# Longformer attention and token mixer, 8 batches: three moves in the turns and scores of batches 1 and 2

## The chip, the cores and the metric

The kernel runs on one core of a Trainium2 chip. The metric is the time of one execution in device microseconds (us), lower is better. The core has a matrix engine (TensorE, PE in the profile, with its weight loads as PEld) and four others that work beside it: VectorE (DVE), ScalarE (ACT), GpSimd (POOL) and SyncE (SP). In this kernel SP only issues transfers, and POOL casts and issues transfers.

## What is computed

Attention with a band of 32 keys to either side and 8 global tokens, then a mixer over the tokens and one over the channels, each with a residual. B=8 batches, H=8 heads, S=576 tokens, D=64.

```python
scores = scale * np.matmul(q, k.transpose(0, 1, 3, 2))
mask = np.abs(pos[:, None] - pos[None, :]) <= window          # window = 32
mask = mask | is_global[:, None] | is_global[None, :]         # 8 global tokens
attn = softmax(np.where(mask, scores, -1e9))
x = (attn @ v)                        # as [8, 576, 512]: the heads side by side
xt = x.transpose(0, 2, 1)
h = np.maximum(xt @ w_tok1, 0.0) @ w_tok2                     # 576 -> 256 -> 576
u = x + h.transpose(0, 2, 1)
h2 = np.maximum(u @ w_ch1, 0.0) @ w_ch2                       # 512 -> 1536 -> 512
return u + h2
```

## The kernel before

Inputs and output are float32, and all matmuls read float16. The 8 heads are worked on as 4 pairs (p = 0 to 3), the 576 tokens as five blocks of 128 (tau = 0 to 4, the last has 64).

There is no loop over batches in time with clean borders. `period(b)` works on two batches at once: the channel products of batch b, and the attention and token mixer of batch n = b + 1, whose loads and casts for batches n + 1 and n + 2 stand there too. The order of the instructions on each engine is the order in which this Python code writes them. The channel products of batch b lie in a list, `dense`: 12 products `M4` (matmuls `b1p`, L713; relu L719 on ACT or L717 on DVE), in odd b three `M4l` for the last 64 tokens of two batches, and per token block two halves of `M5` (six matmuls `op` each, L757; after the second half the sum `osb` on DVE, L761, and its store from SP, L762). `d(k)` writes the next k of them, `d(k, keep)` stops when `keep` are left. So a call of `d` between two steps of the attention puts dense matmuls of batch b between PE instructions of batch n.

The steps of batch n, by their functions, with the names and lines in the profile:

- Casts of q and k: `cast_qk` (L371, tile `qk` from `lq`, `lk`; L368 for the rest of the tokens, `rn` from `lr`). `casts(2, ...)` is a list of nine: the rest, and then q and k of pair 0 (numbers 1, 2), of pair 1 (3, 4), of pair 2 (5, 6), of pair 3 (7, 8). Loads: L88 (`lq`, `lk`), L95 (`lr`), `load_v16` (L360, values).
- Turns: for batches 1 and 2 PE transposes q and k. `T` has eight transposes of one pair into `pT` (L446), `TE_q` and `TE_k` copy them out to `qT` (L450) and `kT` (L456), and `TR` does the rest of the tokens (`pr`, L468 to L470). From batch 3 on transposing transfers do this.
- Scores: `S_all` gives one pair in two PSUM tiles (18 matmuls L486, two exponentials L492 on ACT). `S_two` gives two pairs in three PSUM tiles (36 matmuls L510, four exponentials L516). `SM` masks a pair on DVE (L535, L537 twice).
- Global tokens: `GK` (`gk`, L546 and L547, exponentials `lf`, L549 and L550), `lf_mask` (L557), `OG` (`og`, L564, and `rf` on DVE, L569). `halves` copies values (`vod`, L416 and L418).
- Values: `PV` (`pv`, L590 and L604, normalized on DVE, L619 and L620).
- Token mixer: `M1` (`a1p`, L635, one of five parts each; after the last the relu `a1`, L643, on ACT), `M2` (`hp`, L652, sum `u16`, L657), `M2l` (`hpl`, L664), and `M3_pe` for batch 1 (transposes `pu`, L691, copy `uT`, L693).

PSUM tiles of the attention come from a pool of three buffers (`pss`), those of the dense products from one of two (`psm`). In periods 0 and 1 the scores go pair by pair through `scores(p, k)`, and from batch 3 on through `scores_two(p, k)`. Period 0 is n = 1, period 1 is n = 2.

Of the kernel before, what the change touches and what calls it, by code (L numbers as in the profile page):

```python
# [27 lines left out]
def kernel(  # L28
# [336 lines left out]
    def cast_qk(b, ti, p, eng):  # L365

        if p is None:
            eng(out=rn.rearrange("p n (r d) -> p (n r) d", r=2), in_=lr)  # L368
        else:
            hs = slice(2 * p, 2 * p + 2)  # L370
            eng(out=qk[:, ti, p].rearrange("q i (r d) -> q r i d", r=2), in_=(lq, lk)[ti][:, hs])  # L371
# [41 lines left out]
    def halves(b, cp, c0=0, c1=NT - 1, which=(0, 1)):  # L413
        v0, v1 = vsh[b % 2], vod[b % 2]
        if 0 in which:
            cp(out=v1[0:HB, c0:c1], in_=v0[HB:P, c0:c1])  # L416
        if 1 in which:
            cp(out=v1[HB:P, c0:c1], in_=v0[0:HB, c0 + 1 : c1 + 1])  # L418
# [30 lines left out]
    def TE_q(b, p, copy):  # L449
        copy(  # L450
            out=qTs[b % 2][:, p, 0:4, NG:QS].rearrange("p t (x i) -> p t x i", i=4),
            in_=st[b]["pT", p][:, 0].rearrange("p (i t x) -> p t x i", i=4, t=4),
        )
# [7 lines left out]
    def TE(b, p, copy):  # L461
        TE_q(b, p, copy)
        TE_k(b, p, copy)
# [322 lines left out]
    def period(b):  # L786
# [37 lines left out]

        def scores_two(p, k):
            es = S_two(n, p)
            turned = [] if p else [(f, i) for i in (2, 3) for f in (order_k, order_q)]

            def next_turned():
                if turned:  # L830
                    f, i = turned.pop(0)
                    f(n, i)

            es[0]()
            es[1]()
            next_turned()
            for i in (2, 3):
                d(1)
                es[i]()
                next_turned()  # L840
            SM(n, p)
            d(1)
            next_turned()
            SM(n, p + 1)
            d(1 + k)

        if n > 2:
            scores_two(0, max(tail - 4, 0))
            halves(n, act)
            GK(n)  # L850
            if m < B:
                turns(m)
            d(1)
            lf_mask(n)
            scores_two(2, 1)
        else:
            scores(0, tail > 5)
            scores(1, max(tail - 4 - (tail > 5), 0))
            scores(2, 0)
            GK(n)  # L860
            if n == 2:
                c3 = casts(3, nc.gpsimd.tensor_copy)
                for i in (2, 4):
                    c3[i]()
                load_rest(4, nc.gpsimd)
                for ti in range(2):
                    for i in (5 + ti, 7 + ti):
                        c3[i]()
                    load_qk(4, slice(0, H), nc.gpsimd, slice(ti, ti + 1))
                turns(3)  # L870
            d(1)
            lf_mask(n)
            if n == 1:
                halves(n, dve, 0, 2)
            else:
                halves(n, dve, which=(0,))
            scores(3, 0)
            if n == 1:
                d(1)
            else:  # L880
                halves(n, dve, which=(1,))
            if n == 1:
                c2 = casts(2, nc.scalar.copy)
                for c in c2[0:1] + c2[1::2]:
                    c()
                for p in range(NP):
                    cast_qk(2, 1, p, nc.gpsimd.tensor_copy)
                load(3, nc.sync)
                gather(1)
            else:  # L890
                d(1)
        OG(n)
# [46 lines left out]
            order_q(3, 0)  # L939
        d(1 if n == 1 else len(dense) - (8 + 2 * odd), keep)  # L940
        M1(n, 4)
        d(1, keep)
        if 2 < m < B:
            load_v16(m)
# [10 lines left out]
        if n == 1:  # L955
            d(1, keep)
            M3_pe(1, 0)
            M3_pe(1, 1)
            T(2, 0)
            TE(2, 0, act)  # L960
            TR(2, dve)
            M3_pe(1, 2)
            M3_pe(1, 3)
            T(2, 1)
            d(1, keep)
            TE(2, 1, dve)
            c3 = casts(3, nc.gpsimd.tensor_copy)
            for i in (0, 1, 3):
                c3[i]()
            load_v16(2)  # L970
        else:
            d(1)
            if n == 2:
                order(3, 1)
                gather_c(1)
            d(1)
# [151 lines left out]
```

## Time and profile before

| what | value |
|---|---|
| median of 3 runs | 303.9 us (303.44 to 305.51) |
| profiled execution | 302.77 us, span 300.7 us |
| PE | 289.7 us busy (96%), 2940 matmuls |
| DVE | 180.9 us (60%) |
| ACT | 168.2 us (56%) |
| POOL | 77.3 us (26%) |
| granted TensorE clock | 0.994 |
| transfers | 47.70 MB, mean 159 GB/s |

The profiled execution took 2.07 us more than the span of its instructions. A row of the timeline gives the start in us, the busy time of the group, the engine, the line, the operation with its tiles, shapes and count, and in brackets the idle time ahead of it with what ended it. A row of the list of waits reads: who waited, for whom, us in all, number of waits, mean. A row of the table of stages gives a stretch, its length, the busy us of PE, PEld, DVE, ACT and POOL with the number of instructions, the granted clock, the busy share of the DMA engines and GB/s. Period 0 lies before about 60 us, period 1 from there to about 98 us.

### The profile page before, as it was taken

Reading aid. Unit: us, or ns where it says so; the run is one execution under the profiler, and the core shown is the slowest. Engines: PE = TensorE matmul, PEld = TensorE weight load, DVE = VectorE, ACT = ScalarE, POOL = GpSimd, SP = SyncE. Lnnn points to the kernel's source line nnn. Section 1 sums busy time; section 2 is a strip of 40 time slices with the busy share of each in tenths; the row PEclk is TensorE's granted clock in tenths of the full one; section 3 lists DMA queues with packets and bytes.
Section 4 is the critical chain, followed back from the end, with each engine's and each line's share of the span. In section 5 each row is a group of like instructions: output and inputs, shape, how many; then the busy total and the mean of one; then the engine's idle time right before and its main releaser. Section 6 shows DMA issues by size and latency. Waiting matters only on the chain.

```text
span 300.7 us, 7163 instructions
## 1 busy us (share of the span) xinstructions
PE 289.7 (96%) x2940; PEld 150.0 (50%) x2940; DVE 180.9 (60%) x427; ACT 168.2 (56%) x268; POOL 77.3 (26%) x120
## 2 busy tenths in 40 slices
PE   8869999999999999999999999999999999999994
PEld 7543644354565445444565445444564445444642
DVE  7976698467864845777664755776554766320022
ACT  6785883445638774588539763687343673205500
POOL 8787862289932103200230005000000000000000
PEclk9998999999999999999999999999999999999999
DMA  6999999899999999947993699955502410051013
GB/s 200 238 225 217 264 179 269 233 267 193 239 166 119 150 288 296 164 91 220 297 145 71 177 358 138 91 89 180 101 20 52 159 37 2 17 138 73 0 72 106
DMA packets 106499, 47.70 MB, mean 159 GB/s; under 512 B 84962, under 2 KB 100450, under 8 KB 106466
## 3 DMA queue, kind: packets, MB, share of 16 engines
q1 hardware_dynamic: 67536, 33.18, 48.4%
q0 software_dynamic: 38768, 13.93, 43.9%
q8 instruction: 23, 0.38, 0.6%
q10 hardware_dynamic: 162, 0.13, 0.1%
q14 instruction: 10, 0.08, 0.1%
HBM read 36.11 MB, written 9.44 MB: 151 GB/s over the span
## 4 chain that ended last, share of the span: by engine, by line
PE 84%; DMA 5%; SPq 4%; DVE 3%; ACT 2%; issue 1%; POOLq 0%; ACTq 0%
PE op L757 28%; PE b1p L713 27%; PE a1p L635 5%; PE hp L652 4%; PE b1lp L729 4%; PE pv L590 3%; DMA lq<-in_q_dram 3%; PE pv L604 3%; SPq L102 2%; PE s L510 2%; DMA lv<-in_v_dram 2%; SPq L88 1%; PE pT L446 1%; PE s L486 1%; PE ope L741 1%; PE og L564 1%
## 5 line engine op out<-in xcount | busy, mean ns | idle before, releaser
L713 PE MATMUL b1p<-uT,wc 128*128 128x512 f16 x384 | 92.6, 379 | 0.0
L757 PE MATMUL op<-wc,b 128*128 128x512 f16 x384 | 87.2, 379 | 0.0
L719 ACT ACTIVATE b<-b1p 128x512 f16<-128x512 f32 x84 | 50.2, 598 | 65.6 <-PE b1p L713 50.4
L757 PEld LDWEIGHTS <-b 128*128 128x128 f16 x384 | 36.5, 98 | 43.8 <-issue 1.6
L713 PEld LDWEIGHTS <-wc 128*128 128x128 f16 x384 | 35.3, 98 | 39.5 <-issue 4.0
L360 POOL DMA_DIRECT2D vsh<-in_v_dram x35 | 30.0, 870 | 88.0 <-PE pv L590 76.5
L761 DVE TENSOR_TENSOR osb<-u,op 128x512 f32<-128x512 f16 x32 | 21.9, 685 | 40.4 <-PE op L757 40.4
L657 DVE TENSOR_TENSOR u<-x,hp 128x512 f16<-128x512 f16 x28 | 17.4, 682 | 25.1 <-PE hp L652 25.1
L516 ACT ACTIVATE e_all<-s 128x816 f16<-128x816 f32 (+3 forms) x40 | 24.6, 687 | 7.0 <-issue 4.9
L537 DVE TENSOR_TENSOR e_all<-e_all,bandm 128x616 f16<-128x616 f16 x56 | 24.8, 483 | 1.0
L620 DVE TENSOR_TENSOR x<-pv,rr 128x512 f16<-128x512 f32 x32 | 22.1, 692 | 1.1
L492 ACT ACTIVATE e_all<-s 128x544 f16<-128x544 f32 (+1 forms) x24 | 16.2, 683 | 5.6 <-PE s L486 3.1
L619 DVE RECIPROCAL rr<-pv 128x8 f32<-128x8 f32 (+1 forms) x40 | 8.1, 202 | 17.9 <-PE pv L604 17.7
L371 ACT CAST qk<-lq 128x512 f16<-128x512 f32 x26 | 15.8, 621 | 4.7 <-DMA lq<-in_q_dram 3.8
L635 PE MATMUL a1p<-x,w 128*128 128x512 f16 x64 | 17.5, 392 | 0.0
L590 PEld LDWEIGHTS <-e_all 128*64 128x64 f16 x576 | 12.4, 113 | 8.3 <-issue 6.5
L590 PE MATMUL pv<-vsh,e_all 128*64 128x66 f16 x320 | 14.9, 198 | 0.0
L604 PE MATMUL pv<-rf,lf 128*128 128x264 f16 (+1 forms) x80 | 13.6, 284 | 0.9 <-DVE rf L569 0.8
L371 ACT CAST qk<-lk 128x512 f16<-128x512 f32 x21 | 12.9, 621 | 2.4 <-DMA raw<-qk 1.8
L652 PE MATMUL hp<-a,w 128*128 128x512 f16 x56 | 13.2, 378 | 0.5 <-ACT a L643 0.5
L590 PE MATMUL pv<-vod,e_all 128*64 128x66 f16 x256 | 12.1, 199 | 0.9 <-DVE vod L418 0.9
L717 DVE TENSOR_SCALAR b<-b1p 128x512 f16<-128x512 f32 x12 | 8.3, 691 | 7.4 <-PE b1p L713 6.8
(184 smaller groups left out, 350.5 us busy)
## 6 DMA issues: line engine op xcount, KB each, us to landing
out_dram<-osb SPq DMA_DIRECT2D x32, 256.0 KB, 4.0
lq<-in_q_dram SPq DMA_DIRECT2D x4, 1024.0 KB, 6.5
lk<-in_k_dram SPq DMA_DIRECT2D x4, 1024.0 KB, 7.4
wc<-in_moe_w_ch_dram POOLq DMA_DIRECT2D x6, 512.0 KB, 9.3
vsh<-in_v_dram POOLq DMA_DIRECT2D x21, 128.0 KB, 6.9
lq<-in_q_dram POOLq DMA_DIRECT2D x2, 1024.0 KB, 8.6
lk<-in_k_dram POOLq DMA_DIRECT2D x2, 1024.0 KB, 13.5
vsh<-in_v_dram POOLq DMA_DIRECT2D x14, 96.0 KB, 6.8
```

The lines of the kernel that those rows point to most:

```text
L360: nc.gpsimd.dma_start(out=vsh[b % 2][r0:r1, c, :, 0:D], in_=v[b, :, j0 : j0 + (r1 - r0), :].rearrange("h p d -> p h d"),)
L371: eng(out=qk[:, ti, p].rearrange("q i (r d) -> q r i d", r=2), in_=(lq, lk)[ti][:, hs])
L516: nc.scalar.activation(out=e_all[:, 2 * (p + dp) : 2 * (p + dp) + 2, x0:x1], in_=tiles[t][:, :, o : o + x1 - x0], func=AF.Exp, scale=scale,)
L537: nc.vector.tensor_mul(out=e2[:, par], in0=e2[:, par], in1=bandm)
L590: nc.tensor.matmul(ps[r0 : r0 + HB, hf, VW * hh : VW * hh + VW], lhsT=e_all[:, h, x0 : x0 + HB], rhs=(vsh, vod)[i][b % 2][:, tau, h, :], s ...
L604: nc.tensor.matmul(s["pv", tau][r, hf, 0 : NP * VW], lhsT=s["lf"][:, P * tau : P * tau + (HB if last else P)], rhs=s["rf"][:, 2 * hf : 2 * ...
L620: nc.vector.tensor_tensor(out=x_of(b, tau)[r].rearrange("p (f h x) -> p f h x", f=2, h=NP), in0=pq[r, :, :, 0:D], in1=rr[r].unsqueeze(3).t ...
L635: nc.tensor.matmul(ps[tt], lhsT=w, rhs=x_of(b, ch), start=(ch == 0), stop=(ch == NT - 1))
L652: nc.tensor.matmul(ps[:, i, :], lhsT=w2[:, ch, P * tau : P * tau + P], rhs=s["a1"][:, ch, :], start=(ch == 0), stop=(ch == 1),)
L713: nc.tensor.matmul(ps, lhsT=wc1[:, cc, P * j : P * j + P], rhs=s["uT"][:, cc, :], start=(cc == 0), stop=(cc == 3))
L719: nc.scalar.activation(out=s["b1"][:, j, :], in_=ps, func=AF.Relu)
L757: nc.tensor.matmul(ps, lhsT=w, rhs=wc2[:, j, :], start=(j == 0), stop=(j == NJ - 1))
```

## The change

It has three parts. First, at the end of period 0, the q casts of pairs 2 and 3 of batch 2 (`c2[5]`, `c2[7]`) on ACT, the four k casts on POOL, the load of batch 3 and `gather(1)` are written after `M1(n, 4)`, so the relu of `a1` precedes those casts. Second, also in period 0, one half of `op_2` is written behind `T(2, 0)`, `TE(2, 0)` where it stood behind `T(2, 1)`. Third, batch 2 takes its scores through `scores_two`, in two groups of two pairs, with the turns of pairs 2 and 3 inside the first group; `GK` and the first copy of values come ahead of the second group.

```diff
         def scores_two(p, k):
             es = S_two(n, p)
-            turned = [] if p else [(f, i) for i in (2, 3) for f in (order_k, order_q)]
+            if p:
+                turned = []
+            elif n > 2:
+                turned = [lambda f=f, i=i: f(n, i) for i in (2, 3) for f in (order_k, order_q)]
+            else:
+                turned = [
+                    lambda: None, lambda: (T(n, 2), TE_q(n, 2, dve)), lambda: (TE_k(n, 2, dve), T(n, 3)),
+                    lambda: (TE_q(n, 3, dve), TE_k(n, 3, dve)),
+                ]
...
         else:
-            scores(0, tail > 5)
-            scores(1, max(tail - 4 - (tail > 5), 0))
-            scores(2, 0)
+            if n == 1:
+                scores(0, tail > 5)
+                scores(1, max(tail - 4 - (tail > 5), 0))
+                scores(2, 0)
+            else:
+                scores_two(0, max(tail - 4, 0))
             GK(n)
...
                 halves(n, dve, which=(0,))
-            scores(3, 0)
             if n == 1:
+                scores(3, 0)
                 d(1)
             else:
+                scores_two(2, 0)
                 halves(n, dve, which=(1,))
             if n == 1:
                 c2 = casts(2, nc.scalar.copy)
-                for c in c2[0:1] + c2[1::2]:
-                    c()
-                for p in range(NP):
-                    cast_qk(2, 1, p, nc.gpsimd.tensor_copy)
-                load(3, nc.sync)
-                gather(1)
+                for i in (0, 1, 3):
+                    c2[i]()
             else:
                 d(1)
         OG(n)
...
         M1(n, 4)
+        if n == 1:
+            for i in (5, 7):
+                c2[i]()
+            for p in range(NP):
+                cast_qk(2, 1, p, nc.gpsimd.tensor_copy)
+            load(3, nc.sync)
+            gather(1)
         d(1, keep)
...
             M3_pe(1, 1)
             T(2, 0)
             TE(2, 0, act)
+            d(1, keep)
             TR(2, dve)
             M3_pe(1, 2)
             M3_pe(1, 3)
             T(2, 1)
-            d(1, keep)
             TE(2, 1, dve)
```

ACT at the end of period 0, the piece of the difference around the relu of batch 1 (`a_1` from `a1p`, L643); the numbers behind a name are its buffer's.

```order
 L371 CAST qk<-lq 128x2x4x64 [waits DMASW7_49,Activation_49]
 L371 CAST qk<-lq 128x2x4x64 [waits Activation_49]
+L643 ACTIVATE a_1_1229<-a1p_1172 128x1024 [waits PE_49]
 L371 CAST qk<-lq 128x2x4x64 [waits DMASW1_49,Pool_49]
 L371 CAST qk<-lq 128x2x4x64 [waits Pool_49]
-L643 ACTIVATE a_1_1243<-a1p_1186 128x1024 [waits PE_49]
 L693 COPY uT_1285<-pu_1_1292 128x4x128 [waits PE_49]
```

The relu now stands between the second and the third of the four q casts.

PE from the turns of batch 2 to its first scores, before. Of each group of equal matmuls the first row stands here.

```order
L446 MATMUL pT_2_0_1298<-ident_124,qk_79 128x128 [waits DVE_49]
L468 MATMUL pr_2_1309<-ident_124,rn_80 128x128 [waits Activation_49]
L691 MATMUL pu_1_2_1316<-ident_124,u16_1_1245 128x128 [waits DVE_49]
L691 MATMUL pu_1_3_1322<-ident_124,u16_1_1245 128x128 [waits PE_49]
L446 MATMUL pT_2_1_1328<-ident_124,qk_79 128x128 [waits Activation_49]
L757 MATMUL op_0_2_1337<-wc2_179,b1_0_838 128x512
L486 MATMUL s0_2_0_1354<-qT0_131,kT0_133 128x72 [waits DVE_49]
L486 MATMUL s1_2_0_1363<-qT0_131,kT0_133 128x72 [waits Activation_49]
L757 MATMUL op_0_2_1337<-wc2_179,b1_0_838 128x512
L446 MATMUL pT_2_2_1385<-ident_124,qk_79 128x128 [waits PE_49]
```

The same place of the changed kernel:

```order
L446 MATMUL pT_2_0_1298<-ident_124,qk_79 128x128 [waits DVE_49]
L757 MATMUL op_0_2_1309<-wc2_179,b1_0_838 128x512
L468 MATMUL pr_2_1316<-ident_124,rn_80 128x128 [waits Activation_49]
L691 MATMUL pu_1_2_1323<-ident_124,u16_1_1231 128x128 [waits DVE_49]
L691 MATMUL pu_1_3_1329<-ident_124,u16_1_1231 128x128 [waits Activation_49]
L446 MATMUL pT_2_1_1335<-ident_124,qk_79 128x128 [waits PE_49]
L510 MATMUL s0_2_0_1354<-qT0_131,kT0_133 128x72 [waits DVE_49]
L510 MATMUL s1_2_0_1355<-qT0_131,kT0_133 128x72 [waits Activation_49]
L510 LDWEIGHTS kT0_133 [waits DVE_49]
L510 MATMUL s2_2_0_1356<-qT0_131,kT0_133 128x72 [waits Activation_49]
L757 MATMUL op_0_2_1309<-wc2_179,b1_0_838 128x512
L446 MATMUL pT_2_2_1405<-ident_124,qk_79 128x128
```

The six `op_0_2` matmuls moved from behind `pT_2_1` to behind `pT_2_0`, and 36 score matmuls of two pairs follow `pT_2_1` at once; the weight load that waits for DVE is the first of the second pair.

SP at the end of period 0, the piece of the difference around the store of `osb_0` and the load of batch 3 (`lr`, `lq`, `lk`).

```order
-L95 DMA lr<-in_q_dram 64x8x64 [waits DMAHW4_49,DMASW5_49,Activation_49]
-L95 DMA lr<-in_k_dram 64x8x64 [waits DMAHW5_49,DMASW6_49]
-L88 DMA lq<-in_q_dram 128x8x256 [waits DMAHW2_49,DMASW7_49,DMAHW6_49,DMASW1_49,Activation_49]
-L88 DMA lk<-in_k_dram 128x8x256 [waits DMASW2_49,DMAHW3_49,DMASW0_49,DMAHW7_49,DVE_49,Pool_49]
-L762 DMA out_dram<-osb_0_1238 128x512 [waits DMAHW0_49,DVE_49]
+L762 DMA out_dram<-osb_0_1224 128x512 [waits DMAHW4_49,DVE_49]
+L95 DMA lr<-in_q_dram 64x8x64 [waits DMAHW5_49,DMASW5_49,Activation_49]
+L95 DMA lr<-in_k_dram 64x8x64 [waits DMAHW6_49,DMASW6_49]
+L88 DMA lq<-in_q_dram 128x8x256 [waits DMAHW2_49,DMASW7_49,DMAHW7_49,DMASW1_49,Activation_49]
+L88 DMA lk<-in_k_dram 128x8x256 [waits DMAHW0_49,DMASW2_49,DMAHW3_49,DMASW0_49,Pool_49]
```

Before, this store stood behind those four loads; now it stands ahead of them.

More of the change, by code (lines that the diff above doesn't have):

```diff
@@ L826, in scores_two @@
             es = S_two(n, p)
-            turned = [] if p else [(f, i) for i in (2, 3) for f in (order_k, order_q)]
+            if p:
[7 more added lines that the diff above has]
+                ]
             def next_turned():
                 if turned:
-                    f, i = turned.pop(0)
-                    f(n, i)
+                    turned.pop(0)()
             es[0]()
```

## The prediction

> **What bounds the kernel now.** I read the table of stages first, then PE's list of waits from 50 to 100 us, then the timelines of PE, ACT and DVE between 53 and 83 us, where every moved instruction stands.
>
> ```profile
> 98.00:298.00 200.00, 198.67 (x1806) 98.69 (x1805) 110.05 (x239) 108.33 (x164) 13.50 (x16) 1.00 0.81 131
> PE hp L652 <- ACT a L643: 0.5, 1, 0.5
> PE pu L691 <- DVE kT L470: 0.4, 1, 0.4
> PE s L510 <- DVE qT L398: 0.4, 1, 0.4
> PE pr L468 <- ACT uT L693: 0.2, 1, 0.2
> ```
>
> From 98 us on PE is busy 198.67 of 200 us, and the change touches nothing there. So PE's matmul stream sets the time, and only its gaps in batches 1 and 2 (periods 0 and 1, before 98 us) can be won. The waits there sum to 1.5 us. Removing all of them gains half a per cent; what the change adds must be laid against that.
>
> **The relu.** Before, the relu of `a1` (L643) is queued on ACT behind four casts of q.
>
> ```profile
> 55.25 0.59 PE L635 MATMUL a1p<-xl,w1l 128*128 128x512 f16 x2
> 57.65 1.89 PE L652 MATMUL hp<-a,w 128*128 128x512 f16 x8 [0.52 <-ACT a L643]
> 54.50 2.18 ACT L371 CAST qk<-lq 128x512 f16<-128x512 f32 x4 [2.92 <-DMA lq<-in_q_dram]
> 56.59 1.01 ACT L643 ACTIVATE a<-a1p 128x1024 f16<-128x1024 f32 x1
> ```
>
> The casts wait for q until 54.50, then run to 56.68; the relu's input is complete at 55.84 (55.25 + 0.59). With two casts ahead instead of four, ACT is free at about 55.6, the relu runs from 55.9 to 56.9, and `hp` can start when the half product ahead of it on PE is issued: that began 0.43 after 55.25 and has six matmuls of 0.217, so 57.0. Gain 57.65 - 57.0 = **-0.6** (bounds -0.5 and -0.65). The two late casts end at 57.9 instead of 56.7; their turns on PE come after 67, so they are covered.
>
> **The channel product between the turns.** Six matmuls of `op_2` (a channel product of batch 0) move from behind `pT_1` to behind `pT_0`.
>
> ```profile
> 61.84 0.61 PE L446 MATMUL pT<-ident,qk 128*128 128x128 f16 x8
> 62.61 0.38 PE L468 MATMUL pr<-ident,rn 128*128 128x128 f16 x4 [0.16 <-ACT uT L693]
> 63.58 0.40 PE L691 MATMUL pu<-ident,u 128*128 128x128 f16 x4 [0.36 <-DVE kT L470]
> 63.81 0.61 PE L446 MATMUL pT<-ident,qk 128*128 128x128 f16 x8
> 64.26 1.46 PE L757 MATMUL op<-wc,b 128*128 128x512 f16 x6
> 65.65 0.45 PE L486 MATMUL s<-qT,kT 64*128 64x72 f16 x18
> 66.04 1.47 PE L757 MATMUL op<-wc,b 128*128 128x512 f16 x6
> 67.34 0.61 PE L446 MATMUL pT<-ident,qk 128*128 128x128 f16 x8
> 64.46 0.69 DVE L450 COPY qT<-pT 128x512 f16<-128x512 f16 x1 [0.61 <-PE pT L446]
> 65.07 0.68 DVE L456 COPY kT<-pT 128x512 f16<-128x512 f16 x1
> ```
>
> Start to start, eight transposes take 0.45 and four take 0.23. From 61.84 to 63.81 stand a group of eight and three of four, 1.14 us of work in 1.97: 0.83 of standing, which 1.30 us of product now covers. One wait comes back. `pT_1` now takes the PSUM buffer that `pr` used, and that is free 0.97 after `pr` starts (62.61 to 63.58, released by L470), while PE has 0.69 of transposes in between: +0.28. Net **-0.55** (bounds -0.83 with no wait, -0.3).
>
> **Scores of batch 2 in two groups.** `scores_two` writes 36 score matmuls of two pairs in a row into three PSUM tiles; before, 18 of one pair alternated with products.
>
> *What it saves.* Six product matmuls take 1.39 ahead of scores (64.26 to 65.65) and 1.30 ahead of transposes (66.04 to 67.34): 0.09 for a change of form. There are five such places before (four score groups, one `gk`) and two after, -0.27; and 36 scores in one go take less than twice 0.39 (first row of the next block), -0.1. Together **-0.35** (bounds -0.1, -0.4).
>
> *What it adds first.* The second pair's scores need that pair's kT, which DVE copies out of `pT_1`. Before, two product halves, one score group and another turn lay between; now only the first pair's 18 scores do. By the rows, L456 ends 1.94 after `pT_1` starts (63.81 to 65.07 + 0.68). PE has 0.45 of transposes and 0.39 of scores to do: it stands 1.94 + 0.05 - 0.84 = **+1.15**. Behind it on PE wait the second half of `op_2` and all that follows. The lowest comparable row is the same place in batch 3, below: 0.36. The upper bound adds one more DVE copy of 0.42 to 0.69: 1.7. I take 1.15, since both DVE copies read this very tile.
>
> ```profile
> 140.27 0.66 PE s L510 x36
> 98.29 0.46 PE L510 MATMUL s<-qT,kT 64*128 64x72 f16 x18 [0.36 <-DVE qT L398]
> 71.07 0.69 DVE L761 TENSOR_TENSOR osb<-u,op 128x512 f32<-128x512 f16 x1 [0.63 <-PE op L757]
> 71.68 0.68 DVE L450 COPY qT<-pT 128x512 f16<-128x512 f16 x1
> 74.56 0.29 PE gk L546 x4
> L516 ACT ACTIVATE e_all<-s 128x816 f16<-128x816 f32 x10 | 8.5, 847 | 7.0 <-issue 4.9 <-ACT qk L371 2.1
> L516 ACT ACTIVATE e_all<-s 128x688 f16<-128x688 f32 x10 | 7.5, 749 | 0.0
> L516 ACT ACTIVATE e_all<-s 128x544 f16<-128x544 f32 x10 | 6.4, 636 | 0.0
> L516 ACT ACTIVATE e_all<-s 128x416 f16<-128x416 f32 x10 | 5.2, 517 | 0.0
> 140.36 0.60 ACT L719 ACTIVATE b<-b1p 128x512 f16<-128x512 f32 x1 [0.23 <-ACT lf L550]
> 140.85 1.77 ACT L516 ACTIVATE e_all<-s 128x816 f16<-128x816 f32 x3
> ```
>
> *Then `gk`.* It moves up to just behind `b1p_0`, and its fourth pair needs the last pair's qT. DVE makes that (L450) behind `osb_3`: 0.2 until `osb_3` starts after its product, then 71.07 to 72.36, 1.49 in all. PE has `b1p_0` (four matmuls and a change of form, 0.96) and three quarters of `gk`, at least 0.22. Wait **+0.3** (bounds 0, 0.7).
>
> *Then ACT.* All relus of this period run on ACT (the other periods give two to DVE), two PSUM buffers hold their inputs, and four exponentials now stand among them in one stretch. A relu is followed 0.49 later by the next instruction; the exponentials advance by their means less 0.1: 0.75, 0.42, 0.54, 0.65. From `b1p_1`'s end to the end of `b1p_4`'s relu: 3 x 0.49 + 2.36 + 0.60 + 0.15 of release = 4.6. PE has 36 scores (0.66) and four groups of 0.87, 4.1, before `b1p_6` needs that buffer: **+0.5** (bounds 0, 1.0).
>
> *Last, a wait that goes.* The masks of pairs 2 and 3 now end before the values need `rf`.
>
> ```profile
> 80.45 0.72 DVE rf L569
> 81.21 0.61 PE pv L604 x4
> 145.91 0.63 PE pv L590 x32
> ```
>
> `b1p_7` ends at 80.31, the 32 value matmuls take 0.63, and L604 starts only at 81.21, released by `rf`: 0.27 of standing. In the change the four exponentials end 1.5 us ahead of `og`, so **-0.3** (bounds -0.3, and 0 if the copy of values ahead of these masks on DVE is late).
>
> The sum: -0.6 - 0.55 - 0.35 + 1.15 + 0.3 + 0.5 - 0.3 = **+0.15 us**. The waits that go are paid back by three that come. The profiled execution took 302.77 us (span 300.7 and 2.07 around it), the median of the runs shown is 303.9, 1.1 above; 0.15 on that median is **304.0**.
>
> [...] At 57.65 PE stood 0.52 for `a1` with a product ready behind it. [...]
>
> **Rivals.**
>
> *Faster: the three new waits are small.* If the second pair waits 0.36 as in batch 3 and `gk` and the relus wait nothing, the sum is 0.15 - 0.79 - 0.8 = -1.45: 302.5. For it: the same grouping runs in every later batch, and 98 to 298 us has only 1.3 us of gaps. Against: there q and k come ready from transposing transfers, nothing is turned on PE just ahead, and two relus are on DVE.
>
> *Slower: batch 2's values come late.* SP's first transfer of the next load (L95) left at 51.61; now it stands behind `osb_0`'s store, which waits for DVE until 56.1.
>
> ```profile
> 51.61 0.61 SPq L95 DMA_DIRECT2D lr<-in_q_dram  x1
> lr<-in_q_dram SPq DMA_DIRECT2D x1, 128.0 KB, 6.6
> 65.39 0.62 POOL L368 CAST rn<-lr 128x512 f16<-128x512 f32 x1
> 67.06 4.32 POOL L360 DMA_DIRECT2D vsh<-in_v_dram  x5
> vsh<-in_v_dram POOLq DMA_DIRECT2D x1, 96.0 KB, 6.5
> lk<-in_k_dram POOLq DMA_DIRECT2D x2, 1024.0 KB, 13.5
> 61.30:64.30 3.00, 2.48 (x38) 2.13 (x37) 2.25 (x6) 1.87 (x4) 2.22 (x3) 1.00 0.82 210
> ```
>
> It would leave near 57 and land at 63.9 after 6.6. POOL needs it at 65.39, then issues the values; the last lands at 70.5 + 6.5 = 77.0, and `og` needs it near 79.3. So 1.5 us of slack at POOL and 2.3 at `og`. Past 3.8 us of lateness each us costs one. If it took 13.5 us, as batch 2's k did, it would land 5.1 after 65.39, the values 2.8 after `og`: 306.8. For it: the DMA engines are crowded there. Against: the median and the row above.
>
> *Slower: PE's clock.* The turns now run from `pr` to the second pair's scores with 1.14 of transposes, 0.78 of scores and 1.43 of standing, 3.3 us without a large matmul. If the clock were halved for as long, half of 3.3 is lost: +1.7, 305.7. The last row speaks against it: 1.00 through 3 us of turns and gaps. [...]
>
> *The relu does not move `hp`.* If another wait holds `hp` at 57.65, 0.6 is lost: 304.6. Nothing in PE's waits names one.
>
> **How the numbers follow.** Forecast (within 0.8 of 304.0) 0.70; small waits 0.12; late values 0.07; clock 0.05; relu without effect 0.06. Within 1% (3 us), about what a measurement of this kernel can tell from no change, lie the forecast, the first rival and the last. Slower by over 1% takes the upper part of the two slow cases and a corner of the forecast's: 0.09. Faster by over 1% would need more than all the standing before 98 us: 0.04, for the spread of runs. Same: 0.87. The low end is the first rival with the bounds of the gains on its side: -0.65 - 0.83 - 0.4 + 0.36 - 0.3 = -1.8, 302.1. The high end takes the upper bounds of the three new waits (0.55 + 0.4 + 0.5 more) and of the turns and the values (0.25 + 0.3 more), 304.0 + 2.0 = 306.0, which holds the clock and leaves out most of the late values.
>
> **What would show it.** `hp` with no idle before it at 57.0; `pr` without a wait; PE idle about 1.1 before a score matmul of batch 2, released by DVE kT L456; 0.3 before `gk` (DVE qT L450); small gaps before `b1p_5` and `b1p_6`, released by ACT; `pv` L604 no longer held by `rf`. The forecast is wrong if the wait for L456 is below 0.4 or above 1.7, if `og` waits for values, or if the clock falls below 1.00 between 60 and 80 us.

## The result, and the profile after

| kernel | median | range | executions |
|---|---|---|---|
| before | 303.99 us | 302.65 to 307.18 | 22 |
| changed | 306.66 us | 304.67 to 309.77 | 22 |

The ratio is 1.0071, interval 1.0045 to 1.0098: the changed kernel is slower, by 2.7 us between the medians. The ratio leaves out executions more than 1.5% above the fastest of their kernel, which the medians and ranges keep; by it the loss is about 2.2 us. The forecast was no change that can be measured, 304.0 us, at most 306.0. The profiled execution after took 305.47 us (span 303.5), 2.7 more than the one before. Run three more times beside the kernel before, the change gave 1.0048, 1.0027 and 1.0081 (first experiment).

The table of stages of the changed kernel, for the same 200 us as before, shifted by the 2.7 us that the program is late there:

```profile
100.70:300.70 200.00, 198.65 (x1806) 98.58 (x1805) 109.92 (x239) 107.79 (x163) 12.53 (x15) 1.00 0.74 128
```

Its list of PE's waits from 50 to 102 us:

```profile
PE pT L446 <- DVE kT L470: 1.1, 1, 1.1
PE s L510 <- DVE kT L456: 1.0, 1, 1.0
PE s L510 <- DVE qT L398: 0.4, 1, 0.4
PE gk L546 <- DVE qT L450: 0.3, 1, 0.3
```

The last 200 us are the same as before: 198.65 us of PE against 198.67. Everything happens ahead of them. The wait of `hp` is gone, and three new ones stand in the list. Two of them, for L456 and L450, were expected. The largest, 1.1 us of the next turn for L470, was expected at 0.28.

PE's timeline of the changed kernel, from the relu of batch 1 to the values of batch 2:

```profile
56.59 0.59 PE L635 MATMUL a1p<-xl,w1l 128*128 128x512 f16 x2
58.31 1.89 PE L652 MATMUL hp<-a,w 128*128 128x512 f16 x8
64.24 0.39 PE L468 MATMUL pr<-ident,rn 128*128 128x128 f16 x4
64.47 0.61 PE L691 MATMUL pu<-ident,u 128*128 128x128 f16 x8
66.19 0.62 PE L446 MATMUL pT<-ident,qk 128*128 128x128 f16 x8 [1.12 <-DVE kT L470]
66.75 0.45 PE L510 MATMUL s<-qT,kT 64*128 64x72 f16 x18
68.20 0.45 PE L510 MATMUL s<-qT,kT 64*128 64x72 f16 x18 [1.00 <-DVE kT L456]
75.12 0.32 PE L546 MATMUL gk<-qT,kgz 128*32 128x384 f16 x1 [0.33 <-DVE qT L450]
77.12 4.89 PE L713 MATMUL b1p<-uT,wc 128*128 128x512 f16 x20
81.94 0.47 PE L564 MATMUL og<-vsh,eg 128*32 128x132 f16 x20
83.94 0.51 PE L604 MATMUL pv<-rf,lf 128*128 128x264 f16 x3
```

`hp` starts without idle time, 1.72 after the last part of `a1p` (2.40 before), and `pr` needs no wait. Then PE stands twice, ahead of the second turn and ahead of the second pair's scores. The other engines of the same kernel show why:

```profile
65.65 0.29 DVE L469 COPY qT<-pr 128x256 f16<-128x256 f16 x1 [2.27 <-PE pu L691]
65.74 0.61 POOL L368 CAST rn<-lr 128x512 f16<-128x512 f32 x1 [1.14 <-issue]
67.46 0.68 DVE L456 COPY kT<-pT 128x512 f16<-128x512 f16 x1
```

`pr` was issued at 64.24 and takes 0.39, so DVE could have copied it from about 64.65; L469 starts at 65.65, after 2.27 us of idling. POOL, idle too, starts again 0.09 later. The second standing is as foreseen: L456 ends at 68.14, and the scores start at 68.20.

### The profile page after: what moved, and what is told of

It reads as the page before. It is cut to its first block, busy times and chain, and to the rows that moved or that the text cites. A ratio compares the mean times of both kernels' runs of the same rounds, so it can differ in the third digit from the quotient of the medians.

```text
span 303.5 us, 7162 instructions
## 1 busy us (share of the span) xinstructions
PE 289.9 (96%) x2940; PEld 150.2 (49%) x2940; DVE 182.1 (60%) x427; ACT 168.3 (55%) x268; POOL 77.2 (25%) x120
## 4 chain that ended last, share of the span: by engine, by line
PE 86%; SPq 4%; DVE 4%; DMA 2%; ACT 2%; issue 1%
PE op L757 29%; PE b1p L713 27%; PE a1p L635 6%; PE pv L590 4%; PE hp L652 4%; PE pv L604 4%; PE b1lp L729 4%; DMA lv<-in_v_dram 2%; SPq L102 2%; PE s L510 2%; SPq L88 1%; PE pT L446 1%; PE og L564 1%; PE ope L741 1%; ACT e_all L516 1%
## 5 line engine op out<-in xcount | busy, mean ns | idle before, releaser
L360 POOL DMA_DIRECT2D vsh<-in_v_dram x35 | 29.8, 863 | 90.4 <-PE pv L590 83.0
L516 ACT ACTIVATE e_all<-s 128x816 f16<-128x816 f32 (+3 forms) x48 | 29.8, 689 | 8.6 <-issue 4.9
L604 PE MATMUL pv<-rf,lf 128*128 128x264 f16 (+1 forms) x80 | 13.7, 286 | 0.8 <-issue 0.8
L392 DVE COPY kT<-raw 128x512 f16<-128x512 f16 x20 | 12.2, 610 | 0.0
```

The lines of the kernel that those rows point to most:

```text
L360: nc.gpsimd.dma_start(out=vsh[b % 2][r0:r1, c, :, 0:D], in_=v[b, :, j0 : j0 + (r1 - r0), :].rearrange("h p d -> p h d"),)
L516: nc.scalar.activation(out=e_all[:, 2 * (p + dp) : 2 * (p + dp) + 2, x0:x1], in_=tiles[t][:, :, o : o + x1 - x0], func=AF.Exp, scale=scale,)
L604: nc.tensor.matmul(s["pv", tau][r, hf, 0 : NP * VW], lhsT=s["lf"][:, P * tau : P * tau + (HB if last else P)], rhs=s["rf"][:, 2 * hf : 2 * ...
```

## Where the time goes: one balance for three executions

The window from the last part of `a1p` to `pv` L604 holds all moved work. It is cut at `hp`, at `pT_1` (the second turn) and at `og`; the product half that moved from the third piece to the second is counted in the third (1.30 us). Each number is the piece's length less that of before, from the starts in the timelines. The column "undisturbed" is an execution of the same changed kernel from the third comparison, the last one from the fourth. All are held against the one profiled execution of before.

| piece | predicted | undisturbed | profiled after | fourth |
|---|---|---|---|---|
| relu, to `hp` | -0.6 | -0.54 | -0.68 | -0.67 |
| turns, `hp` to `pT_1` | -0.55 | -0.56 | +0.42 | +1.22 |
| scores, `gk`, relus, to `og` | +1.6 | +1.70 | +1.92 | +3.24 |
| `og` to `pv` L604 | -0.3 | -0.26 | -0.27 | -0.26 |
| sum | +0.15 | +0.34 | +1.39 | +3.53 |

The rows of `og` before, and of the undisturbed execution on PE:

```profile
78.94 0.47 PE L564 MATMUL og<-vsh,eg 128*32 128x132 f16 x20
```

```profile
55.65 0.59 PE L635 MATMUL a1p<-xl,w1l 128*128 128x512 f16 x2
57.51 0.81 PE L652 MATMUL hp<-a,w 128*128 128x512 f16 x3
63.44 0.39 PE L468 MATMUL pr<-ident,rn 128*128 128x128 f16 x4
64.41 0.62 PE L446 MATMUL pT<-ident,qk 128*128 128x128 f16 x8
66.42 0.45 PE L510 MATMUL s<-qT,kT 64*128 64x72 f16 x18 [1.00 <-DVE kT L456]
79.94 0.47 PE L564 MATMUL og<-vsh,eg 128*32 128x132 f16 x20
81.95 0.62 PE L604 MATMUL pv<-rf,lf 128*128 128x264 f16 x4
```

Here `pT_1` follows `pr` after 0.97, and every piece is within 0.1 us of its forecast. The remaining profile of the change, from the second comparison, is like it (-0.67, -0.55, +1.71, -0.27, in sum +0.22). So the sum was right for an execution in which nothing comes late, which holds for two of the four profiles, and the wait of 0.9 to 1.0 for L456 is there in all four. The fourth comparison's execution shows what the sum left out, in its timeline, on PE, ACT, DVE and POOL:

```profile
63.90 0.39 PE L691 MATMUL pu<-ident,u 128*128 128x128 f16 x4
66.20 0.38 PE L691 MATMUL pu<-ident,u 128*128 128x128 f16 x4 [1.92 <-ACT kT L456]
68.42 0.69 PE L510 MATMUL s<-qT,kT 64*128 64x72 f16 x18 [0.89 <-DVE kT L456]
69.04 2.74 PE L757 MATMUL op<-wc,b 128*128 128x512 f16 x6
65.08 0.59 ACT L450 COPY qT<-pT 128x512 f16<-128x512 f16 x1 [2.43 <-PE pu L691]
65.19 0.29 DVE L469 COPY qT<-pr 128x256 f16<-128x256 f16 x1 [2.37 <-PE pu L691]
65.28 0.61 POOL L368 CAST rn<-lr 128x512 f16<-128x512 f32 x1 [1.39 <-issue]
```

and in its table of stages, right behind:

```profile
69.00:72.50 3.50, 3.50 (x20) 1.61 (x17) 0.68 (x2) 1.54 (x3) 3.50 (x6) 0.61 1.86 182
```

There is first a late restart: ACT, DVE and POOL all stand for 1.4 to 2.4 us and start again within 0.2 us of each other. ACT's copy needs only `pT_0`, which was done before 62.7; in the undisturbed execution it starts 0.65 after `pT_0` starts, here 3.15. What the three share is that each waits for PE: ACT for `pT_0`, DVE for `pr`, and POOL's cast writes `rn`, which `pr` reads. PE then stands 1.92. Second, the granted clock: right behind the two standings it is 0.61 over 3.5 us, and six product matmuls take 2.74 where 1.46 is usual. The two together are the 3.2 us between this execution and the undisturbed one.

## The experiments

All ratios are against the kernel before, measured in the same rounds on the same chip. Its median was 302.8 in the first group, then 304.5, 302.6, 304.6 and 304.1.

**The change again**, three times (no edit): how much the ratio itself varies.

> The change as it is, a second execution. Theory W (PE's waits between 57 and 82 us are the loss): +1.4 us over the kernel before in the stretch from the first b1p of batch 0 to the end, with waits of about 1.0 before the second pair's scores and 0.3 to 0.8 in gk. The wait of 1.1 for L470 before the turn of pair 1 comes again if it belongs to the order of the instructions, and shrinks to 0.3 if the 0.9 us between PE's pr and DVE's copy of it was chance. Rival S (the start is slower too): the first b1p of batch 0 starts near 33.9 again, 1.6 later than before, and the time is +2.2 or more.

> The change as it is, beside the three below on one chip. Its profiled executions so far: +0.2 and +1.4 us between the last a1p parts of batches 1 and 2 (36.28 and 37.46 against 36.06), where the runs say +1.4 to +2.1 in the median. Theory E (exposed waits): the wait for L456 of about 1.0 is there again, and PE's standing in the turns varies from execution to execution by up to 2 us.

> The change as it is, a fourth time. Three ratios so far: 1.0071, 1.0048, 1.0027. If the waits that the profiles show are the loss, 36.3 to 36.4 us between the last a1p parts in an execution without late signals, up to 37.5 with them, and a ratio of 1.001 to 1.007: the higher, the more the kernel before is disturbed on this chip too.

Measured 304.04 (1.0048, interval 1.0017 to 1.0078), 304.09 (1.0027, 0.9999 to 1.0055) and 306.37 (1.0081, 1.0048 to 1.0114). The change is slower by 0.3 to 0.8%, though the interval of the third comparison just takes in no change. The wait of 1.1 for L470 was not there in the second and third profile, so it does not belong to the order of the instructions. The loss is larger where the kernel before is slower too (304.1 and 304.0, against 302.6 and 302.8). The start before the window varies by as much as the loss: the first `b1p` of batch 0 stood at 33.85, 33.49, 30.83 and 32.97 in the four profiles, and at 32.29 in the one of before.

**Each part alone.** The three edits are the three parts of the diff above, one at a time; one or two lines stand for each.

```diff
 # the relu alone
-                for c in c2[0:1] + c2[1::2]:
+                for i in (0, 1, 3):
 # the product half alone
             TE(2, 0, act)
+            d(1, keep)
...
-            d(1, keep)
 # the two groups alone
+                scores_two(0, max(tail - 4, 0))
```

> Only the first part: the relu ahead of two q casts, with the POOL casts, the load of batch 3 and the gathers behind it. Theory W: hp starts about 1.7 instead of 2.4 after the last a1p, -0.7 us. Rival L (the moved transfers cost): no gain or a loss, with a wait of PE for values or for q and k of batch 2 or 3 before 98 us, +1 us or more.

> Only the second part: six op matmuls behind the turn of pair 0 instead of pair 1. If the wait of 1.1 for L470 belongs to this order: +0.3 to +0.5 us, the wait is there again, and PE stands again before the first pair's scores (none to 0.3 for qT, kT). If that wait was chance: -0.5 to 0.

> Only the third part: batch 2's scores in two groups, with the op half still between the turn of pair 1 and the scores. Theory W: the second pair's kT is ready (1.94 us after the turn's start, against 2.2 us of PE work), so no wait for L456; gk waits 0.3 to 0.8, relus 0.4, against 0.3 saved in changes of form and 0.3 at rf: 0 to +0.5 us. Rival G (the grouping itself is the loss): +1.5 us or more, with the wait for L456 there.

> The third part alone, one more look at another execution. Of its 12 runs 6 were above 304.9 us where the profiled one took 302.8; an execution above 304.9 would show in its profile what is late: theory D (transfers): DVE or PE wait for transposed q and k (raw) or values between 75 and 135 us; rival C (clock): a second stretch at half clock; rival I: PE's signals or instructions come late without a wait in the program.

Measured: relu 302.58 (1.0004, 0.9970 to 1.0038); product half 302.48 (0.9987, 0.9961 to 1.0013); two groups 304.50 (1.0042, 1.0001 to 1.0084); two groups once more, a single time, 305.64 beside a median of 304.5. PE's timeline of the product half alone, of the two groups alone, and of the two groups once more:

```profile
63.15 0.39 PE L468 MATMUL pr<-ident,rn 128*128 128x128 f16 x4
64.12 0.62 PE L446 MATMUL pT<-ident,qk 128*128 128x128 f16 x8
64.67 0.45 PE L486 MATMUL s<-qT,kT 64*128 64x72 f16 x18
65.06 1.47 PE L757 MATMUL op<-wc,b 128*128 128x512 f16 x6
```

```profile
63.61 0.61 PE L446 MATMUL pT<-ident,qk 128*128 128x128 f16 x8
64.06 1.46 PE L757 MATMUL op<-wc,b 128*128 128x512 f16 x6
65.45 0.73 PE L510 MATMUL s<-qT,kT 64*128 64x72 f16 x36
```

```profile
67.49 0.27 PE L510 MATMUL s<-qT,kT 64*128 64x72 f16 x6 [0.39 <-ACT uT L693]
68.32 0.45 PE L510 MATMUL s<-qT,kT 64*128 64x72 f16 x18 [0.56 <-DVE kT L456]
```

In the first profiles neither part has the wait for L456. With the product half moved but scores taken pair by pair, a product half follows one pair's scores. With scores in two groups but the half in its old place, the half stands between `pT_1` and the 36 scores, which run through. One half covered two waits in turn; the change takes it for one, and the other stays bare. In the second execution of the two groups, with a late restart in the turns, the half is not cover enough, and 0.56 of the wait is back. Nor do the times settle this part: at 1.0042 the two groups alone cannot be told from the whole change beside them (1.0048). In the relu's run `hp` starts 1.73 after `a1p` without idle time, but the 0.7 us that its expectation named does not show in the time (1.0004, give or take 1 us). In its profiled execution PE stands for 3.9 us between 125 and 140 us, so only its rows ahead of that are read.

**Two parts at a time.** The changed kernel without the product half's move, and without the relu's.

```diff
 # relu and two groups: the product half back
             T(2, 1)
+            d(1, keep)
 # product half and two groups: the casts back ahead of the relu
+                for c in c2[0:1] + c2[1::2]:
```

> First and third part together (relu ahead, two groups of scores), the op half still behind the turn of pair 1. By PE's waits between 55 and 92 us: the relu's -0.7 and the groups' +0.3, so -0.4 us. Theory T (the third part makes executions with late events more frequent, whose place no profile has shown so far): median +1 us or more, and a wait of more than 1 us somewhere after the start that the kernel before does not have. Rival S (the loss is in the start before 32 us, by chance of the executions): -0.4 to 0 with the start as in the kernel before.

> Second and third part together, the relu and the loads of batch 3 as before. By PE's waits: -0.5 (turns), +1.1 (L456 before the second pair), +0.6 (gk and relus), less 0.6 (forms, rf): +0.6 us. Theory T: median +1.5 us or more. If the moved load of batch 3 is needed for the loss: not more than +0.6.

Measured 305.62 (1.0011, 0.9975 to 1.0047) and 307.48 (1.0086, 1.0050 to 1.0121). The pair that shares the one half is the slow one, without the relu's move too; the product half alone and the other pair cannot be told from no change, and the lower end of the two groups alone is 1.0001. That slow pair lost 2.6 us where the waits gave 0.6, so the moved load of batch 3 is not needed for the loss. Relu and two groups has both signs of theory T in its profile and median (a wait of 1.8 in the turns, 1.1 above the kernel before), but its interval holds no change. The profiled execution of product half and two groups, PE's timeline, and then two stretches of its table of stages:

```profile
68.12 0.27 PE L510 MATMUL s<-qT,kT 64*128 64x72 f16 x6 [1.26 <-ACT uT L693]
68.95 0.58 PE L510 MATMUL s<-qT,kT 64*128 64x72 f16 x18 [0.56 <-DVE kT L456]
69.46 2.74 PE L757 MATMUL op<-wc,b 128*128 128x512 f16 x6
```

```profile
69.13:72.55 3.42, 3.42 (x30) 1.68 (x23) 0.30 (x1) 1.67 (x3) 3.42 (x5) 0.50 1.36 139
65.00:69.10 4.10, 1.84 (x44) 1.35 (x43) 2.20 (x5) 1.34 (x2) 3.79 (x7) 1.00 1.13 289
```

Half the clock for 3.42 us, behind 4.1 us in which PE was busy for 1.84.

**The relu on DVE**, with the product half's move: is the gain at `hp` lost to what ACT does next?

```diff
+        if b == 1:
+            nc.vector.tensor_scalar(out=a1, in0=s["a1pp"], scalar1=0.0, scalar2=None, op0=ALU.max)
```

> Second part, and the relu of a1 of batch 1 on DVE, which stands idle there, in place of ACT; casts and loads keep their places, the scores go pair by pair. hp starts about 1.8 after the last a1p instead of 2.4, and the turns save 0.8: -0.8 to -1.0 us by PE's waits, with no rise of late executions.

Measured 305.27 (1.0014, 0.9978 to 1.0049). `hp` starts 2.08 after the last part of `a1p`: 0.32 better than before, 0.35 worse than the change's order on ACT. The 0.8 to 1.0 us expected did not show.

**Cover for the second pair's scores.** One product half is put between the scores of the two pairs (and the first of the loop behind them left out), or 32 matmuls of zeros, which add work and take no wait away.

```diff
         for dp, t, o, x0, x1 in parts:
+            if b == 2 and p == 0 and dp == 1 and t == 1:
+                d(1)
 # or
+                for _ in range(32):
+                    nc.tensor.matmul(tiles[2][:, 0, 400:464], lhsT=wz, rhs=wz[:, 0:64], start=True, stop=True)
```

> The whole change, but one half of op_2 stands between the scores of the first and the second pair of batch 2, and the turn of pair 2 follows the second pair's scores at once. Theory E: the wait for L456 is gone (1.0 us), PE stands less than 0.3 before these scores even in an execution with late signals, and the time is 1.0 to 2.0 us below the whole change's, at or below the kernel before. Rival G (grouping costs for another reason, the DVE or ACT queues behind it): no more than 0.5 us below the whole change's.

> The whole change with the op half between the scores of the first two pairs, on another chip: below the kernel before again (its ratio was 0.9963). Its one profile so far had a wait of 1.3 in gk behind a mask that took 2.2 us; theory M: that was one execution's, and the wait is 0 to 0.8 here.

> The whole change with 32 more matmuls of zeros (128x64, into columns that nobody reads) in the place where PE waits for L456. They take about 0.9 us of a wait of 1.0, so by the waits alone the time is that of the whole change, +0 to +0.3. Theory C (part of the loss is the clock that is halved for 3.4 us behind the standing, as in the run of the second and third part at 69.1 us): executions with a granted clock of 0.989 or less get as rare as in the kernel before, and the time falls by 0.5 us or more.

Measured: cover 302.44 (0.9963, 0.9937 to 0.9988) and again 305.20 (1.0000, 0.9964 to 1.0037); zeros 304.04 (1.0041, 1.0019 to 1.0062). In the rounds in which the change itself gave 1.0027, the cover is 1.65 us below it. PE, DVE and POOL of the cover's first profiled execution (line numbers are two higher):

```profile
64.78 1.47 PE L759 MATMUL op<-wc,b 128*128 128x512 f16 x6
66.18 0.45 PE L512 MATMUL s<-qT,kT 64*128 64x72 f16 x18
72.79 0.32 PE L548 MATMUL gk<-qT,kgz 128*32 128x384 f16 x1 [1.31 <-DVE qT L450]
68.66 2.89 DVE L539 TENSOR_TENSOR e_all<-e_all,bandm 128x616 f16<-128x616 f16 x2
69.65 1.23 POOL L371 CAST qk<-lk 128x512 f16<-128x512 f32 x2
70.76 0.77 POOL L95 DMA_DIRECT2D lr<-in_q_dram  x1
```

The wait for L456 is gone. But `gk` now waits 1.31 for DVE: the two masks ahead of its copy take 2.89 in place of 0.87, and the long one ends at 71.5, when POOL's casts and its transfer's issue end. So in the two profiled executions of these rounds the cover's window, from `a1p` to `pv`, is 26.39 us and the change's 26.30: the 1.65 us between the medians is not seen in it. The zeros start only after a wait of 0.90 of their own and shift the scores by 0.93; the time is that of the change. No execution with the zeros had a granted clock of 0.989 or less, and yet none of the 0.5 us of theory C was won. The cover run again lost its lead: 1.0000 against 0.9963, with no wait in the window (25.22 us), but a mean granted clock of 0.983 in its profiled execution (0.994 in the cover's first).

**The masks after the copies.** The turned copies of pairs 2 and 3, and the sum for `osb_3`, go ahead of the first two masks on DVE, without and with the cover.

```diff
+            if n == 2 and p == 0:
+                next_turned()
+                d(1)
+                SM(n, p)
```

> The whole change, with DVE's copies of the turn of pair 3 and the sum osb_3 ahead of the masks of pairs 0 and 1 in batch 2. Theory M (masks that take longer while POOL works stand ahead of the copy that gk needs): gk no longer waits (0.3 to 0.8 before), also where a mask takes 1 to 2 us; 0.3 to 1.0 us below the whole change, the wait of 1.0 for L456 stays. Rival: masks are late for og then, and og or the values wait as long as gk did; no change.

> The whole change with both repairs, the op half between the scores of the first two pairs and the masks behind the copies. Both waits (L456 1.0, gk 0.3 to 1.3) gone: by PE's waits -0.9 to -1.5 us against the kernel before, and the lowest of all versions. If lateness in the turns is the whole of the loss and masks are none of it: the same as with the half alone.

> The version with both repairs once more, beside the whole change on one chip. Its profile had no wait for L456 and none in gk, but 1.2 us of late signals in the turns, so 36.10 us between the last a1p parts; without them 34.9 is expected, 1.2 below the kernel before and 1.4 to 1.5 below the whole change. In the runs: ratio 0.995 to 0.999 against the kernel before.

Measured 305.87 (1.0045, 1.0005 to 1.0085), 304.03 (0.9983, 0.9939 to 1.0027) and 304.11 (1.0010, 0.9982 to 1.0038). No profile of the three lists a wait of `gk`, so this edit takes away what it names; alone it leaves the kernel slower than before, although the window of its profiled execution (25.62 us) is shorter than that of before (25.96). What the waits gave for both repairs together, 0.9 to 1.5 us below the kernel before, did not show in either run. PE of the last one:

```profile
66.96 0.56 PE L512 MATMUL s<-qT,kT 64*128 64x72 f16 x18
67.46 1.47 PE L759 MATMUL op<-wc,b 128*128 128x512 f16 x6
68.86 0.45 PE L512 MATMUL s<-qT,kT 64*128 64x72 f16 x18
73.70 0.36 PE L548 MATMUL gk<-qT,kgz 128*32 128x384 f16 x4
```

Beside the change in the same rounds, the two forms of cover are lower by 1.65 (304.09 to 302.44), 1.84 (305.87 to 304.03, both with late masks) and 2.26 us (306.37 to 304.11). In the first and the last pair the intervals do not overlap. Each difference is more than the wait of 1.0 that the cover hides, but the excess lies within the noise of 1 to 2 us.

**The cover without the relu's move**, and with the relu on DVE.

```diff
 # product half, two groups, cover; the casts stay ahead of the relu
+                for c in c2[0:1] + c2[1::2]:
 # the same with the relu on DVE
+        if b == 1:
+            nc.vector.tensor_scalar(out=a1, in0=s["a1pp"], scalar1=0.0, scalar2=None, op0=ALU.max)
```

> As the one before, but relu, casts and the load of batch 3 in their old places. The relu's wait of 0.2 to 0.5 ahead of hp comes back: +0.3 to +0.7 against the one before. If the moved load of batch 3 has a cost of its own (late transfers), this one is the same or lower.

> The relu of a1 of batch 1 on DVE (casts and loads in their old places), the op half behind the turn of pair 0, the scores in two groups with the op half between the pairs. By PE's waits: relu -0.3 to -0.7, turns -0.5, forms -0.3, rf -0.3, gk and relus +0.6 to +1.0: -0.8 us against the kernel before. If transfers of batch 3 need to be late for the loss, this one is better than the one with the cover alone; otherwise the same within 0.5 us.

Measured 305.21 (0.9991, 0.9948 to 1.0033) and 303.84 (1.0018, 0.9981 to 1.0056). With the cover the harmful pair is back at no change (1.0086 without it, in other rounds); the relu's place cannot be told at this scale, and neither the 0.3 to 0.7 us that its old place should cost nor the 0.8 us that the last version should win was seen.

**The clock over all executions.** Each execution has a mean granted clock. In the profiled one of before it is 0.50 from 21.4 to 24.7 us and 1.00 from 24.8 on, in all 0.994; in the changed one 0.50 from 24 to 26 us, in all 0.993. Of the 20 profiled executions 12 lie at 0.992 to 0.994, three at 0.999 or 1.000 and five at 0.989 or less. The fourth of the change, at 0.987, has two such stretches: 0.72 from 18 to 24 us and 0.61 from 69 to 72.5. That 0.989 or less stands for a second stretch in the other executions too is an estimate from these numbers: half of 3.3 us is 0.0055 of 300.7.

| kernels | 0.989 or less | median of these | of the others |
|---|---|---|---|
| before | 30 of 156 | 306.1 | 303.5 |
| the change | 17 of 56 | 307.0 | 304.9 |
| product half and two groups | 7 of 12 | | |
| change, late masks | 6 of 12 | | |
| cover, four runs | 6 of 48 | 307.4 | 303.9 |
| cover without the relu's move, two runs | 5 of 24 | | |
| zeros | 0 of 12 | | |

Where the two pairs' scores stand bare, 30 of 80 executions have 0.989 or less, against 30 of 156 before and 11 of 72 with a product half there. The executions come from several chips: in four groups of rounds the bare scores have it more often than the kernel before, in the third less often (1 of 12 against 7 of 36). In most executions the place of the low clock was not profiled. Of the five profiled ones with 0.989 or less, three show a slow stretch right behind the turns: the fourth of the change (0.61 over 3.5 us), product half and two groups (0.50 over 3.42) and, with a product half between the scores, the cover without the relu's move (at 68.85 six product matmuls take 2.21 where 1.46 is usual). With late masks, at 0.987, the six take 1.46 or 1.47 from 57 to 74 us, so the place is elsewhere; for the cover run again, at 0.983, it is not shown. And the change is slower without it too: among executions above 0.989 by 0.7, 1.5 and 1.5 us in the three groups that hold both kernels. So the second stretch is a part of the loss where it falls behind the turns, but not the whole of it.

## Why the prediction was wrong

*The relu, right, in part by luck.* Forecast -0.6; -0.54 to -0.68 against the one profile of before. But what the old order costs depends on where PE is when q lands. With the casts in their old place, `hp` starts 1.73 after `a1p` where `a1p` is late (two groups once more, 56.17; cover without the relu's move, 57.25) and 3.11 after it where `a1p` is early (two groups alone, 54.34), so the gain lies between 0 and 1.4 us. In the profiled execution of the change the casts start at 54.47. All four would have ended at 56.65 (2.18 later, as before), ahead of the relu's input at 57.18: by this estimate the old order would have cost nothing there.

*The turns: the step that failed, as far as the profiles show.* "`pT_1` now takes the PSUM buffer that `pr` used, and that is free 0.97 after `pr` starts": that 0.97 was one reading of before, and the bounds (-0.83, -0.3) allowed it to change by no more than 0.3. In the undisturbed execution it is again 0.97, and the net -0.56 against -0.55. In the profiled one it is 1.95 and in the fourth 2.75, since ACT, DVE and POOL restart late. That term was -0.55 with a narrow range and came out between -0.56 and +1.22. The late restart does not come from the moved half: in relu and two groups, with the half behind `pT_1` as before, the turns took 1.41 longer than before as well. So neither the bounds of this term nor the high end of 306.0, which adds 0.25 for the turns, had room for an execution with late signals.

*The wait for L456, right.* Forecast 1.15; 1.00 in the profiled, the second and the undisturbed execution, 0.89 in the fourth. The term takes for granted that the product half behind the waiting scores does not run ahead of them, and so it was: in all four it starts behind the second pair's scores (68.58 behind 68.20, 67.41 behind 67.02, 66.80 behind 66.42 and 69.04 behind 68.42).

*`gk`, too small.* Forecast 0.3, bounds 0 and 0.7. The list of waits has 0.33 in the profiled execution and nothing in the undisturbed one, but from the first `gk` to the product behind the last it takes 0.40 before (74.49 to 74.89), 0.95 undisturbed (72.55 to 73.50) and 1.16 in the profiled one (74.33 to 75.49): +0.55 and +0.76. With the cover the listed wait grew to 1.31, past the upper bound, which had no lengthened mask in it.

*The relus behind the exponentials, right.* 20 matmuls of `b1p` take 4.82 (77.12 to 81.94); at 0.217 each and 0.09 for the change of form they would take 4.43: +0.39 against 0.5.

*The values, right.* `pv` L604 starts 2.00 after `og` (2.27 before), and nothing waits for late values: POOL's cast stands at 65.74 where 65.39 was before.

*The clock, under-rated.* The rival was "3.3 us without a large matmul", +1.7, chance 0.05. The fourth execution has it at that place and near that price (six matmuls 1.27 late, the piece 1.5), and 30 of 80 executions have a mean of 0.989 or less. The row of before that spoke against it (1.00 from 61.3 to 64.3 us) was for a stretch in which PE was busy 2.48 of 3.00 us; after, PE is busy 1.81 of 3 us from 66 to 69.

```profile
66.00:69.00 3.00, 1.81 (x46) 1.32 (x47) 1.76 (x4) 1.66 (x4) 3.00 (x5) 1.00 1.38 252
```

The profiled execution kept 1.00 even so, while product half and two groups, busy 1.84 of 4.10 us, had 0.50 for the next 3.42. So such a gap was followed by the half clock in some executions only, and no run shows what decides it; +1.7 was the author's estimate.

So of 2.7 us, the sum accounts for 0.2 to 0.3 in an undisturbed execution, the late restart for 1.0 to 1.8 where it occurs, and the half clock for about 1.5 where it occurs. The profiled execution's other 1.3 us lie ahead of 56 us, before the window (`a1p`'s last part at 56.59, before 55.25), where all kernels vary by as much.

Three things stay open. First, what makes three engines restart late. It is in profiles of several orders, some with the turns as before (relu and two groups: 1.8 us ahead of the second `pu`), and in none of the first and third groups of rounds, where the kernel before is some 1.5 us faster. A transfer of instructions falls between 64.3 and 64.9 us, in the gap, in the profiled execution; but between 55 and 80 us there are two such transfers in it, in the fourth, in the undisturbed one, where all engines run on time, and before, so their number does not decide. Second, the change is 1.2 and 1.5 us slower in the first and third groups too, where its profiles give 0.2 to 0.3 and show no late restart: about 1 us there has no place in any profile. Third, no profile of the kernel before was taken in these rounds, so it is not shown how often each event hits it. The median's 2.7 us is therefore not summed to the end.

## What to carry to other kernels

A block of independent work that can be moved is often the cover of the wait behind it as well: before it is taken for one gap, count what the waits behind it cost without it. Two moves that use the same block can cost more together (1.0086) than the one alone (0.9987); the other one alone, at 1.0042, is not settled here. A cover sized to the undisturbed latency (0.28 of standing left) is no cover for a latency that varies by 1 to 2 us between executions (0.97, 1.95 and 2.75 from `pr` to `pT_1`). A product half between two standings was worth 1.6 to 2.3 us in the medians here, against a listed wait of 1.0. The matrix engine's clock, which fell behind two such standings in two profiled executions (0.50 over 3.42 us, 0.61 over 3.5) and by the matmuls' times in a third (2.21 where 1.46 is usual), is one reason for that where it occurs; it is not shown to be the whole. And a sum of waits from one profile of each kernel is no forecast of the medians to less than 1 us where executions of one kernel spread over 4.5 us (302.65 to 307.18): the waits gave the repaired versions gains of up to 1.5 us, and one of their six runs came out clearly below the kernel before.

## What the hardware showed beside that

- In the fourth execution ACT, DVE and POOL started again at 65.08, 65.19 and 65.28 after idling 2.43, 2.37 and 1.39 us. By PE's rows `pT_0`, for which ACT waited, was done at 62.54, and `pr`, for which DVE and POOL waited, at 64.06. No wait of the program accounts for ACT's delay. For POOL the row of the landing of `lr` is missing, so a late transfer is not ruled out there.
- With the cover a mask on DVE (two f16 inputs of 128x616) took 2.17 us in place of 0.48 while POOL cast and issued a transfer. It ended at 71.55, so began at 69.38, ahead of POOL's casts at 69.65, but POOL was issuing transfers when it began (L360, 65.39 to 69.72). Which part of POOL's work goes with the stretched mask, the rows do not settle.
- The list of waits names the last instruction before a release (DVE kT L470, 1.1 us). That DVE was not the cause is seen only one step further back, in the 2.27 us for which DVE itself idled ahead of L469.
